# Seven block products in place of eight in one output stage

## The chip, the core and the metric

The kernel runs on one NeuronCore of a Trainium2 chip. The core has a matrix engine (TensorE, PE in the profile, with PEld for its weight loads), a vector engine (VectorE, DVE), a scalar engine (ScalarE, ACT), a general-purpose engine (GpSimd, POOL) and a queue engine (SyncE, SP). Sixteen DMA engines move data within the on-chip memory SBUF and between it and DRAM (matmul results lie in a separate memory, PSUM); the engine that issues a transfer waits first for what the transfer needs. Each engine works through its own instructions in the order in which the program gives them, and engines wait for each other by semaphores.

The metric is the device time of one execution in microseconds (us), given as the median of several runs.

## The reference

The input x has 2048 rows (time steps) of 512 bf16 numbers. With xn the layer norm of x over each row, the output is

```
out = x + y(xn) + f(xn)
y   = 2 Re( h C^T ) + xn * Dskip     with  h[t] = Lam_bar * h[t-1] + B_bar xn[t]     (512 complex states)
f   = ( silu(xn Wg) * (xn Wu) ) Wd                                                    (512 -> 1376 -> 512)
```

All matrices are bf16. Only one product of these is touched by the change: the product of the states h (real and imaginary part side by side, 1024 numbers for each time step) with the folded output matrix, for one quarter of the time steps.

## The kernel before

The 2048 rows are worked in four chunks of 512 time steps (c = 0 to 3), each chunk in four tiles of 128 rows (n = 0 to 15). For a chunk there are these stages:

- `bproj_chunk(c)`: eight tiles of 128 states by 512 steps (real and imaginary part of 512 states), each four matmuls (L380), copied out of PSUM by ScalarE (L382).
- On VectorE, queued as small steps in a backlog: a rotation (L390, L400, L404), eight scans (L422) and a rotation back, which writes the states of the chunk to the tile `wt` (a tensor of 128 x 2 x 4 x 512: the state's row in its block, real or imaginary part, four blocks of 128 states, 512 steps).
- `gateup_chunk(c)`: eleven column tiles of the gate and up products (L455, and L513 for a last mixed tile); ScalarE applies silu to the one (L474) and copies the other (L475), VectorE multiplies two tiles at a time (L470).
- `out_chunk(c)` and, for chunks 2 and 3 together, `out_pair(2)`: for each of four row tiles ten matmuls with the down matrix into one PSUM bank (`out_ffn`, L592, L566), then the remaining 96 rows of the down product (`out_rows`, L555), then `out_ssm` (L604): eight matmuls of 128 x 512 into the same bank, the states in `wt` against the folded output matrix `CF` (128 x 2 x 4 x 512).

The order on each engine is what the program's order of calls makes of it: the code is recorded in this order and is not reordered. The stages around the change follow each other so: `bproj_chunk(2)`, `out_chunk(0)`, `gateup_chunk(2)`, `bproj_chunk(3)`, `load_rows()`, `out_chunk(1)`, `gateup_chunk(3)`, `out_pair(2)`. VectorE's backlog is worked off between the matmul stages by `pump`, which is given the estimated time of the matmuls just recorded; `need(tag)` empties it up to a tag, and `multiply` records the waiting L470 products.

Three shared resources matter here.

PSUM has eight banks, and every matmul group takes one. `out_chunk(0)` leaves its four banks unfinished: the rest of its down product is added only in `out_chunk(1)`, by `out_rows`. So from `out_chunk(0)` to `out_chunk(1)` four banks are left for all other products. In `out_chunk(1)`, the eight banks hold the eight row tiles of chunks 0 and 1; after `out_rows` ScalarE empties the four of chunk 0 (`out_leave`, L617), and after `out_ssm` those of chunk 1.

POOL's queue issues the transfers that add to what is at the destination, and small moves: 48 moves that lay the last 96 gate-times-up rows into `gu_rows` (L188, twelve for each chunk; those of chunks 0 to 2 are issued one after the other), the four loads of `load_rows` (L182), which bring the last 96 rows of the down matrix into a part of the then unused tile `BT` (called `wd_rows` in the code, and read by `out_rows`), and the output stores that add to DRAM (L618, L542). The transfers of this queue use eight semaphores in turn, and POOL issues one only when the transfer eight places earlier has landed.

SBUF tiles that are free by the second half are `CT` (the raw output matrix), `part_end` and `jidx` (float tables), and three buffers `cm`.

Of the kernel before, what the change touches and what calls it, by code (L numbers as in the profile page):

```python
# [10 lines left out]
F32 = mybir.dt.float32  # L11
BF16 = mybir.dt.bfloat16
ALU = mybir.AluOpType
ACT = mybir.ActivationFunctionType
# [9 lines left out]
def kernel(  # L24
# [17 lines left out]
    nc = tc.nc  # L42
    _, L, D = A_x.shape
# [4 lines left out]
    HW = CW // 2  # L48
    NT = L // 128
    NCH = L // CW  # L50
    TPC = CW // 128
    KD = D // 128
    HK = KD // 2
    NQ = Pst // 128
# [11 lines left out]
    ssm = ctx.enter_context(tc.tile_pool(name="ssm", bufs=1))  # L66
    gut = ctx.enter_context(tc.tile_pool(name="gut", bufs=2))
    up_p = ctx.enter_context(tc.tile_pool(name="up_p", bufs=4))
    opool = ctx.enter_context(tc.tile_pool(name="opool", bufs=6))
# [4 lines left out]
    def bank(shape=(128, CW), dtype=F32):  # L74
        return psum.tile(list(shape), dtype, name="ps")

    def flat(ap3):
        return ap3.rearrange("p q j -> p (q j)")

    x_v = A_x[0].rearrange("(n p) d -> p n d", p=128)  # L80
    out_v = out[0].rearrange("(n p) d -> p n d", p=128)
# [17 lines left out]
    CT = const.tile([128, 2, NQ, D], BF16, name="CT")  # L99
# [3 lines left out]
    CF = const.tile([128, 2, NQ, D], BF16, name="CF")  # L103
# [12 lines left out]
    HD = D // 2  # L116
# [51 lines left out]
    jidx = const.tile([128, CW], F32, name="jidx")  # L168
# [7 lines left out]
    part_end = const.tile([128, D], F32, name="part_end")  # L176
# [95 lines left out]
    V = nc.vector  # L272
# [99 lines left out]
    u_tiles, w_tiles = {}, {}  # L372
    car = {}

    def bproj_tile(c, part, q):
        if c not in u_tiles:
            u_tiles[c] = ssm.tile([128, 2, NQ, CW], BF16, name="u16", bufs=2)
        ps = bank()
        for k in range(KD):
            nc.tensor.matmul(ps[:], lhsT=BT[:, part, k, q * 128:(q + 1) * 128], rhs=xnT[:, k, c * CW:(c + 1) * CW],  # L380
                             start=(k == 0), stop=(k == KD - 1))
        nc.scalar.copy(out=u_tiles[c][:, part, q, :], in_=ps[:])  # L382
# [65 lines left out]
    gu_tiles = {}  # L448
# [9 lines left out]
    def gu_tile(c):  # L458
        if c not in gu_tiles:
            gu_tiles[c] = gut.tile([128, FT - 1, CW], BF16, name="guT")  # L460
        return gu_tiles[c]

    def u_tile(c, fi):
        if (c, fi // 2) not in u_pair:
            u_pair[c, fi // 2] = up_p.tile([128, 2, CW], BF16, name="u2")
        return u_pair[c, fi // 2]

    def product(c, fi):
        g, u = gu_tile(c)[:, fi - 1:fi + 1, :], u_tile(c, fi)[:]
        products.append(lambda: V.tensor_tensor(out=g, in0=g, in1=u, op=ALU.mult))  # L470
# [50 lines left out]
    def gateup_tile(c, fi):  # L521
        if fi == FT - 1:
            return gateup_last(c)
        psg = bank()
        gu_mm(psg, wg_g, c, fi, 0, CW)
        psu = bank()
        gu_mm(psu, wu_g, c, fi, 0, CW)
        gu_out(c, fi, psg, psu)
# [16 lines left out]
    o_tiles = {}  # L545

    def out_blocks(n):

        return ((0, D // 2), (D // 2, D - 128), (D - 128, D)) if n == NT - 1 else ((0, D),)

    def out_rows(c, step):

        for i in range(TPC):
            n, rows = c * TPC + i, slice(i * RT, (i + 1) * RT)
            nc.tensor.matmul(o_tiles[n][0][:], lhsT=gu_rows[c][rows, step, :], rhs=wd_rows[rows, step, :],  # L555
                             start=False, stop=(step == 2 and (c == 0 or n == NT - 1)))

    def out_pair(c):

        multiply(0)  # L560
        for n in range(c * TPC, (c + 2) * TPC):
            o = bank()
            o_tiles[n] = [o]
            k, i = divmod(n, TPC)
            for fi in range(FT - 1):
                nc.tensor.matmul(o[:], lhsT=gu_tiles[k][:, fi, i * 128:(i + 1) * 128], rhs=wd_sb[:, fi, :],  # L566
                                 start=(fi == 0), stop=False)
            pump(FT * 0.2163)
        for step in range(3):
            for k in (c, c + 1):  # L570
                out_rows(k, step)
        need(f"ssm{c}")
        need("skip")
        for n in range(c * TPC, (c + 1) * TPC):
            out_ssm(n)
            pump(2 * NQ * 0.2163)
        need(f"ssm{c + 1}")
        n = NT - 1
        o = o_tiles[n][0]
        V.tensor_tensor(out=part_end[:], in0=o[:], in1=xn_end[:, TPC - 1, :], op=ALU.add)  # L580
        o_tiles[n] = [bank((128, hi - lo)) for lo, hi in out_blocks(n)]
        for n in range((c + 1) * TPC, (c + 2) * TPC):
            out_ssm(n)

    def out_ffn(n):
        c, i = divmod(n, TPC)
        o_tiles[n] = []
        for lo, hi in out_blocks(n):
            o = bank((128, hi - lo))
            o_tiles[n].append(o)  # L590
            for fi in range(FT - 1):
                nc.tensor.matmul(o[:], lhsT=gu_tiles[c][:, fi, i * 128:(i + 1) * 128], rhs=wd_sb[:, fi, lo:hi],  # L592
                                 start=(fi == 0), stop=False)

    def out_ssm(n):
        c, i = divmod(n, TPC)
        if c > 0:
            res = opool.tile([128, D], BF16, name="res")
        for o, (lo, hi) in zip(o_tiles[n], out_blocks(n)):
            fresh = n == NT - 1  # L600
            o = o[:, 0:hi - lo]
            for part in range(2):
                for q in range(NQ):
                    nc.tensor.matmul(o, lhsT=w_tiles[c][:, part, q, i * 128:(i + 1) * 128],  # L604
                                     rhs=CF[:, part, q, lo:hi], start=(fresh and part == 0 and q == 0),
                                     stop=(c > 0 and part == 1 and q == NQ - 1))
            if c == NCH - 1:
                rest = part_end[:, lo:hi] if fresh else xn_end[:, i, lo:hi]
                V.tensor_tensor(out=res[:, lo:hi], in0=o, in1=rest, op=ALU.add)  # L609
                for a, b in ((0, D // 2), (D // 2, D)) if i == 0 else ((lo, hi),):  # L610
                    late = b == D and n in (NT - TPC, NT - 1)
                    (nc.sync if late else nc.scalar).dma_start(out=out_v[:, n, a:b], in_=res[:, a:b])
            elif c > 0:
                out_leave(n, o, res)

    def out_leave(n, o, res):
        nc.scalar.copy(out=res[:], in_=o[:])  # L617
        nc.gpsimd.dma_start(out=out_v[:, n, :], in_=res[:], accum_op=ALU.add)  # L618
# [3 lines left out]
    backlog = []  # L622
    owed = [0.0]
# [9 lines left out]
    def step():  # L633
        for item in backlog[0:AHEAD + 1]:
            if item[2] is not None:
                item[2]()
                item[2] = None
        cost, op, _, _ = backlog.pop(0)
        op()
        owed[0] -= cost  # L640

    def pump(us):

        owed[0] += us
        while backlog and owed[0] >= backlog[0][0] * 0.5:
            step()
        if not backlog:
            owed[0] = 0.0

    def multiply(keep):  # L650

        while len(products) > keep:
            products.pop(0)()
            owed[0] -= 0.65

    def need(tag):

        while any(item[3] == tag for item in backlog):
            step()
# [135 lines left out]
    for fis in (range(4, EARLY - 1), range(EARLY - 1, EARLY)):  # L795
        ps, n = bank(), len(fis)
# [4 lines left out]
        pump(GU * n / 4)  # L801
        multiply(1)

    def bproj_chunk(c):
        need(f"ln{c}")
        for part in range(2):
            for q in range(NQ):
                bproj_tile(c, part, q)
                pump(BP)
                multiply(0 if q else 1)  # L810

    def gateup_chunk(c):
        for fi in [FT - 1, *range(FT - 1)]:
            gateup_tile(c, fi)
            pump(GU)
            multiply(1)

    def out_chunk(c):

        multiply(0)  # L820
        for n in range(c * TPC, (c + 1) * TPC):
            out_ffn(n)
            pump(FT * 0.2163)
        if c == 0:
            need("ln3")
            up_halves()
            multiply(0)
        if c == 1:
            for step in range(3):
                for k in range(2):  # L830
                    out_rows(k, step)
            for n in range(TPC):
                out_leave(n, o_tiles[n][0], opool.tile([128, D], BF16, name="res"))
        need(f"ssm{c}")
        need("cf")
        for n in range(c * TPC, (c + 1) * TPC):
            out_ssm(n)
            pump(2 * NQ * 0.2163)
# [12 lines left out]
    def queue_ssm(c):  # L851
        fwd, back = ssm_ops(c)
        queue(f"ssm{c}", fwd + back)
# [31 lines left out]
    nc.sync.dma_start(out=out[0, 0:(NT - TPC) * 128, :], in_=A_x[0, 0:(NT - TPC) * 128, :])  # L885
    queue_ssm(2)
    out_chunk(0)
    gateup_chunk(2)
    bproj_chunk(3)
    load_rows()  # L890
    for c in range(NCH):
# [36 lines left out]
```

## Time and profile before

| | |
|---|---|
| time, median of 3 runs | 178.35 us (178.13, 178.35, 178.47) |
| span of the profiled execution (first to last instruction) | 176.8 us; the profile gives no other time of that execution |
| time outside the span, by the median | 1.5 us |
| TensorE busy | 172.1 us (97%) |
| VectorE busy | 153.8 us (87%) |
| ScalarE busy | 96.4 us (55%) |
| POOL busy | 51.8 us (29%) |
| `gateup_chunk(2)` | 81.2 to 99.4 us |
| `bproj_chunk(3)` | 99.4 to 106.3 us |
| `out_chunk(1)`: down product, `out_rows`, `out_ssm` | 106.3 to 114.8, to 116.3, 116.5 to 123.3 us |
| granted TensorE clock | full (1.000) |

Times in the profile are microseconds from the start of the span. A line of the timeline gives the start, the duration, the engine, the source line, the operation, output and inputs, how many instructions are merged (x), and in brackets how long the engine had been idle and for what it had waited. For POOL the duration of a transfer's line is the time that POOL needs to issue it, not the time of the transfer; the time from issue to landing stands in the list of transfers.

### The profile page before, as it was taken

How to read it: one execution, taken by the hardware profiler on the slowest of the kernel's cores; microseconds unless marked ns; L12 is line 12 of the kernel's file. 1: busy time of each engine (PE TensorE's matmuls, PEld its weight loads, DVE VectorE, ACT ScalarE, POOL GpSimd, SP SyncE). 2: the span in 40 equal slices, each digit the busy share in tenths (PEclk: the TensorE clock that was granted, in tenths of full speed). 3: DMA queues.
4: the chain of work that ended last, by engine and by line, in shares of the span. 5: the costliest groups of instructions: out<-in, count | busy, mean ns of one | idle time of the engine just before them, and what ended most of it. 6: DMA issues, size and time to landing. Idle time of an engine off the chain costs nothing.

```text
span 176.8 us, 2598 instructions
## 1 busy us (share of the span) xinstructions
PE 172.1 (97%) x939; PEld 83.4 (47%) x954; DVE 153.8 (87%) x235; ACT 96.4 (55%) x178; POOL 51.8 (29%) x86
## 2 busy tenths in 40 slices
PE   8999999999999999999999999999999999999993
PEld 3877544444444444444444444444444444444443
DVE  4779998999999997999999999999999999981033
ACT  5397899867698679714666661053866610001300
POOL 6050120001400220019998040058476510001410
PEclk9999999999999999999999999999999999999999
DMA  5998497995431013900000020029799300000652
GB/s 164 305 186 197 91 247 97 336 272 117 88 73 21 0 30 89 356 4 17 17 19 19 0 85 7 0 23 126 88 126 188 64 6 0 0 4 0 64 99 75
DMA packets 31292, 16.36 MB, mean 92 GB/s; under 512 B 20208, under 2 KB 31088, under 8 KB 31248
## 3 DMA queue, kind: packets, MB, share of 16 engines
q1 hardware_dynamic: 24704, 11.51, 27.5%
q0 software_dynamic: 5184, 4.07, 16.0%
q10 hardware_dynamic: 1392, 0.62, 1.2%
q8 instruction: 7, 0.11, 0.3%
q14 instruction: 5, 0.04, 0.1%
HBM read 8.33 MB, written 5.24 MB: 77 GB/s over the span
## 4 chain that ended last, share of the span: by engine, by line
PE 94%; DMA 2%; issue 1%; SPq 0%; DVE 0%
PE ps L455 35%; PE ps L604 16%; PE ps L380 16%; PE ps L566 10%; PE ps L592 10%; DMA wu<-in_B_w_up_dram 2%; PE ps L693 2%; PE ps L513 2%; PE ps L774 2%; PE ps L555 2%; PE ps L502 1%; PE ps L245 0%; SPq L113 0%; SPq L123 0%; DVE res L609 0%
## 5 line engine op out<-in xcount | busy, mean ns | idle before, releaser
L455 PE MATMUL ps<-xnT,wu 128*128 128x512 bf16 (+1 forms) x144 | 36.3, 373 | 0.2
L455 PE MATMUL ps<-xnT,wg 128*128 128x512 bf16 (+1 forms) x145 | 36.3, 373 | 0.2
L422 DVE TENSOR_TENSOR_SCAN g<-r_t,car,u 128x512 bf16<-128x512 f32 x24 | 28.8, 1263 | 0.0
L380 PE MATMUL ps<-xnT,BT 128*128 128x512 bf16 x126 | 28.2, 379 | 0.1
L604 PE MATMUL ps<-CF,wt 128*128 128x512 bf16 (+2 forms) x140 | 27.6, 355 | 0.4 <-issue 0.3
L474 ACT ACTIVATE guT<-ps 128x512 bf16<-128x512 f32 (+1 forms) x40 | 23.6, 590 | 5.9 <-PE ps L455 5.8
L475 ACT CAST u<-ps 128x512 bf16<-128x512 f32 (+1 forms) x40 | 23.0, 576 | 6.5 <-PE ps L455 6.4
L617 ACT CAST res<-ps 128x512 bf16<-128x512 f32 x12 | 6.7, 590 | 36.1 <-PE ps L604 26.8
L455 PEld LDWEIGHTS <-wu 128*128 128x128 bf16 x148 | 14.5, 98 | 16.6
L188 POOL DMA_DIRECT2D gu_rows<-ul x36 | 17.7, 499 | 15.8 <-DVE ul L490 15.8
L455 PEld LDWEIGHTS <-wg 128*128 128x128 bf16 x148 | 14.4, 98 | 16.5
L382 ACT CAST u<-ps 128x512 bf16<-128x512 f32 x32 | 18.2, 586 | 6.0 <-PE ps L380 5.9
L618 POOL DMA_DIRECT2D out_dram<-res x12 | 10.5, 1221 | 36.2 <-ACT res L617 36.1
L604 PEld LDWEIGHTS <-wt 128*128 128x128 bf16 x144 | 13.3, 98 | 15.0 <-issue 1.3
L380 PEld LDWEIGHTS <-BT 128*128 128x128 bf16 x128 | 12.5, 98 | 14.9 <-issue 0.3
L214 POOL TENSOR_TENSOR rstd<-ve,neg_half 128x2 f32<-128x2 f32 (+1 forms) x4 | 5.7, 1418 | 44.9 <-DVE ve L213 44.9
L592 PE MATMUL ps<-wd_sb,guT 128*128 128x512 bf16 x79 | 17.5, 379 | 0.1
L566 PE MATMUL ps<-wd_sb,guT 128*128 128x512 bf16 x79 | 17.4, 379 | 0.1
L470 DVE TENSOR_TENSOR guT<-guT,u 128x1024 bf16<-128x1024 bf16 x20 | 13.4, 678 | 0.0
L566 PEld LDWEIGHTS <-guT 128*128 128x128 bf16 x80 | 7.8, 98 | 9.5
L592 PEld LDWEIGHTS <-guT 128*128 128x128 bf16 x80 | 7.8, 98 | 9.5
L205 DVE BATCH_NORM_STATS2 stats<-xall 128x6 f32<-128x512 bf16 x14 | 9.5, 678 | 2.7 <-DMA xall<-in_A_x_dram 2.7
(125 smaller groups left out, 201.4 us busy)
## 6 DMA issues: line engine op xcount, KB each, us to landing
out_dram<-in_A_x_dram SPq DMA_DIRECT2D x1, 1536.0 KB, 6.9
out_dram<-res POOLq DMA_DIRECT2D x12, 128.0 KB, 3.5
out_dram<-xall POOLq DMA_DIRECT2D x3, 512.0 KB, 8.4
wd_sb<-in_B_w_down_dram SPq DMA_DIRECT2D x2, 640.0 KB, 8.2
xall<-in_A_x_dram SPq DMA_DIRECT2D x1, 1024.0 KB, 7.1
gu_rows<-ul POOLq DMA_DIRECT2D x36, 8.0 KB, 1.6
wg<-in_B_w_gate_dram SPq DMA_DIRECT2D x1, 512.0 KB, 4.7
wu<-in_B_w_up_dram SPq DMA_DIRECT2D x1, 512.0 KB, 5.5
```

The source lines that it names most:

```text
L188: nc.gpsimd.dma_start(out=gu_rows[c][i * RT:(i + 1) * RT, p, :], in_=product[p * RT:(p + 1) * RT, i * 128:(i + 1) * 128])
L380: nc.tensor.matmul(ps[:], lhsT=BT[:, part, k, q * 128:(q + 1) * 128], rhs=xnT[:, k, c * CW:(c + 1) * CW], start=(k == 0), stop=(k == KD - 1))
L382: nc.scalar.copy(out=u_tiles[c][:, part, q, :], in_=ps[:])
L422: V.tensor_tensor_scan(out=g()[:, part, q, :], data0=r_t[:, q:q + 1].to_broadcast([128, CW]), data1=u_tiles[c][:, part, q, :], initial=ini ...
L455: nc.tensor.matmul(ps[:fs, lo:hi], lhsT=wslice(groups, fi, k), rhs=xnT[:, k, c * CW + lo:c * CW + hi], start=(k == 0), stop=(k == KD - 1))
L470: products.append(lambda: V.tensor_tensor(out=g, in0=g, in1=u, op=ALU.mult))
L474: nc.scalar.activation(out=gu_tile(c)[:, fi, 0:hi], in_=psg[:, 0:hi], func=ACT.Silu)
L475: nc.scalar.copy(out=u_tile(c, fi)[:, fi % 2, 0:hi], in_=psu[:, 0:hi])
L566: nc.tensor.matmul(o[:], lhsT=gu_tiles[k][:, fi, i * 128:(i + 1) * 128], rhs=wd_sb[:, fi, :], start=(fi == 0), stop=False)
L592: nc.tensor.matmul(o[:], lhsT=gu_tiles[c][:, fi, i * 128:(i + 1) * 128], rhs=wd_sb[:, fi, lo:hi], start=(fi == 0), stop=False)
L604: nc.tensor.matmul(o, lhsT=w_tiles[c][:, part, q, i * 128:(i + 1) * 128], rhs=CF[:, part, q, lo:hi], start=(fresh and part == 0 and q == 0 ...
L618: nc.gpsimd.dma_start(out=out_v[:, n, :], in_=res[:], accum_op=ALU.add)
```

## The change

Only the state product of chunk 1 (`out_ssm` for n = 4 to 7) is changed; chunks 0, 2 and 3 keep theirs. The product is one of 512 steps x 1024 states with 1024 states x 512 outputs. It is cut into 2 x 2 blocks: A11, A12, A21, A22 are the halves of the steps (256 each) by real and imaginary part, B11, B12, B21, B22 the parts by halves of the outputs (256 each). Strassen's identity in Winograd's form takes seven block products in place of eight, of sums of blocks:

```
S1 = A21 + A22   S2 = S1 - A11   S3 = A11 - A21   S4 = A12 - S2
T1 = B12 - B11   T2 = B22 - T1   T3 = B22 - B12   T4 = T2 - B21
```

What is added:

- The sums of the weights T1 to T4, written over `CT` (`weight_sums`). Each sum starts with a signed copy by ScalarE, in two halves of 128 x 512 elements, and a transfer on POOL's queue that adds the second block. Ten such copies (eight for T1 to T4, two for -B22 in `part_end`) and five transfers (T4 takes two, the second adds B21; signs are chosen so that only additions are needed), each of 128 x 4 x 256 bf16, 256 KB in pieces of 512 bytes. They are recorded two steps after each tile of `gateup_chunk(2)`.
- The sums of the states S1 to S4 (`state_sums`), in the three `cm` buffers and in `jidx`: eight copies and four transfers, recorded one step after each tile of `bproj_chunk(3)`, four after each row tile of `out_ffn`, and the rest before the products; S2 adds S1, and S4 adds S2, in one contiguous piece of 2 KB for each partition.
- The seven block products (`out_ssm_seven`): each eight matmuls of 128 x 256. Four go to banks of their own, three are added to the row tiles' banks.
- ScalarE copies two of the four to SBUF; VectorE forms the sums of the products in four additions of 128 x 512 in f32 and writes the four results (in place of ScalarE's L617) in four more; the stores are unchanged.

On POOL's queue the built program has this order: 24 `gu_rows` moves; the T3 transfer; 12 `gu_rows` moves; T1, T2, T4 first part, T4 second part, S1, S3; the four `wd_rows` loads; S2, S4; then the stores.

```diff
+    BQ = [[CF[:, j, :, h * HD:(h + 1) * HD] for h in range(2)] for j in range(2)]
+    TQ = [CT[:, i // 2, :, (i % 2) * HD:(i % 2 + 1) * HD] for i in range(4)]
+    neg_b22 = part_end[:].bitcast(BF16).rearrange("p (q j) -> p q j", q=NQ)
+    def signed_copy(out, in_, sign):
+        for lo in range(0, NQ, 2):
+            yield lambda lo=lo: nc.scalar.activation(out=out[:, lo:lo + 2], in_=in_[:, lo:lo + 2], func=ACT.Copy,
+                                                     scale=sign)
+    def added(out, in_):
+        yield lambda: nc.gpsimd.dma_start(out=out, in_=in_, accum_op=ALU.add)
+    def weight_sums():
+        (b11, b12), (b21, b22) = BQ
+        t1, t2, t3, t4 = TQ
+        for out, in_, sign, to, add in ((t3, b12, -1.0, t3, b22), (t1, b11, -1.0, t1, b12), (t2, b11, 1.0, t2, t3),
+                                        (t4, b22, -1.0, t4, t1), (neg_b22, b22, -1.0, t4, b21)):
+            yield from signed_copy(out, in_, sign)
+            yield from added(to, add)
...
+    def state_sums(c):
+        (a11, a12), (a21, a22) = state_quarters(c)
+        s1, s2, s3 = (ssm.tile([128, NQ, HW], BF16, name="cm", bufs=3) for _ in range(3))
+        s4 = jidx[:].bitcast(BF16).rearrange("p (q j) -> p q j", q=NQ)
+        s_tiles[c] = (s1, s2, s3, s4)
+        for out, in_, sign, to, add in ((s1, a21, 1.0, s1, a22), (s3, a21, -1.0, s3, a11), (s2, a11, -1.0, s2, s1),
+                                        (s4, a12, -1.0, s4, s2)):
+            yield from signed_copy(out, in_, sign)
+            yield from added(to, add)
+    def out_ssm_seven(c):
...
+        def product(a, b, place, start, stop):
+            for i in range(2):
+                for q in range(NQ):
+                    nc.tensor.matmul(place(i), lhsT=a[:, q, i * 128:(i + 1) * 128], rhs=b[:, q, :],
+                                     start=(start and q == 0), stop=(stop and q == NQ - 1))
...
+        product(a12, b21, at(0, 0), False, False)
+        one = taken(a11, b11)
+        nc.scalar.copy(out=low[:, :, 0], in_=one[:])
+        x = taken(s1, t1)
+        nc.scalar.copy(out=five, in_=x[:])
+        six = taken(s2, t2)
+        step()
+        step()
+        add(u2, six[:], low[:, :, 0])
+        add(low[:, :, 1], u2, five)
+        seven = taken(s3, t3)
+        product(a22, t4, at(1, 0), False, True)
+        product(s4, neg_b22, at(0, 1), False, True)
+        add(high[:, :, 0], seven[:], u2)
+        add(high[:, :, 1], high[:, :, 0], five)
+        finish(1, high)
+        finish(0, low)
+        pump(4 * 2 * NQ * 0.2163)
...
     def bproj_chunk(c):
...
+                spend(1, c == NCH - 1)
     def gateup_chunk(c):
...
+            spend(2)
     def out_chunk(c):
...
+            if c == 1:
+                spend(4, True)
...
         need(f"ssm{c}")
         need("cf")
+        if c == 1:
+            spend(99, True)
+            return out_ssm_seven(c)
...
     out_chunk(0)
+    sums += [*weight_sums(), None]
     gateup_chunk(2)
```

More of the change, by code (lines that the diff above doesn't have):

```diff
@@ new lines, in state_quarters @@
+    def state_quarters(c):
+        w = w_tiles[c]
+        return [[w[:, j, :, h * HW:(h + 1) * HW] for j in range(2)] for h in range(2)]
+    s_tiles = {}
+    def state_sums(c):
[7 more added lines that the diff above has]
+            yield from added(to, add)
@@ new lines, in out_ssm_seven, with at, taken, add @@
+    def out_ssm_seven(c):
+        (a11, a12), (a21, a22) = state_quarters(c)
+        (b11, b12), (b21, b22) = BQ
+        (s1, s2, s3, s4), (t1, t2, t3, t4) = s_tiles[c], TQ
+        first = c * TPC
+        space = flat(gu_tiles[c][:]).bitcast(F32).rearrange("p (s j) -> p s j", j=HD)
+        high, low = (space[:, a:a + 4].rearrange("p (i h) j -> p i h j", h=2) for a in (2, 6))
+        u2, five = high[:, :, 1], space[:, 0:2]
+        def product(a, b, place, start, stop):
[3 more added lines that the diff above has]
+                                     start=(start and q == 0), stop=(stop and q == NQ - 1))
+        def at(half, h):
+            return lambda i: o_tiles[first + 2 * half + i][0][:, h * HD:(h + 1) * HD]
+        def taken(a, b):
+            x = bank((128, 2, HD))
+            product(a, b, lambda i: x[:, i, :], True, True)
+            return x
+        def add(out, in0, in1):
+            V.tensor_tensor(out=out, in0=in0, in1=in1, op=ALU.add)
+            owed[0] -= 0.69
+        def finish(half, extra):
+            for i in range(2):
+                n = first + 2 * half + i
+                res = opool.tile([128, D], BF16, name="res")
+                add(res[:], o_tiles[n][0][:], extra[:, i].rearrange("p h j -> p (h j)"))
+                nc.gpsimd.dma_start(out=out_v[:, n, :], in_=res[:], accum_op=ALU.add)
+        product(a12, b21, at(0, 0), False, False)
[16 more added lines that the diff above has]
+        pump(4 * 2 * NQ * 0.2163)
@@ L802, with spend @@
         multiply(1)
+    sums = []
+    def spend(n, late=False):
+        while n and sums:
+            if sums[0] is None:
+                if not late or any(item[3] == "ssm1" for item in backlog):
+                    return
+                sums[0:1] = state_sums(1)
+            sums.pop(0)()
+            n -= 1
     def bproj_chunk(c):
```

## The prediction

> **What bounds the kernel now.** I read the page's totals first, then the chain that ended last in order of time.
>
> ```profile
> span 176.8 us, 2598 instructions
> ...
> PE 172.1 (97%) x939; PEld 83.4 (47%) x954; DVE 153.8 (87%) x235; ACT 96.4 (55%) x178; POOL 51.8 (29%) x86
> ...
> PE 94%; DMA 2%; issue 1%; SPq 0%; DVE 0%
> ```
>
> ```profile
> 10.52 5.20 PE ps L455 x32
> 15.72 3.13 PE ps L774 x56
> ...
> 99.36 6.91 PE ps L380 x32
> ...
> 107.83 7.07 PE ps L592 x32
> 114.90 1.41 PE ps L555 x24
> 116.31 0.16 issue
> 116.47 6.86 PE ps L604 x31
> 123.32 0.86 PE ps L513 x4
> ...
> 160.29 10.74 PE ps L604 x49
> ```
>
> The columns of the chain are start, duration, and what with how many instructions. TensorE carries the chain from 6 us to the end without a gap over 0.2 us, so a microsecond of matmul time saved, or of stall added, arrives at the end as one. The stage that is changed runs from 116.47 for 6.86 us. VectorE is 87% busy, but holds 0% of the chain: nothing on it is waited for at the end.
>
> **Removed from the path: matmul time.** The chain gives the spacing of back-to-back matmuls by width: 6.91 / 32 = 0.216 us for 512 columns (at 99.36), 5.20 / 32 = 0.1625 for 384 (at 10.52), 3.13 / 56 = 0.056 for 128 (at 15.72). That is proportional to the columns, so 256 columns take 0.108. The stage had 32 x 0.216 = 6.9 us and gets 7 products x 8 matmuls x 0.108 = 6.05: **0.86 us saved**. Each narrow matmul still needs its weights loaded:
>
> ```profile
> L604 PEld LDWEIGHTS <-wt 128*128 128x128 bf16 x144 | 13.3, 98 | 15.0 <-issue 1.3
> ```
>
> 0.098 us is under 0.108, so the loads stay hidden, though barely; were they not, 56 x 0.01 would be the price of each 10 ns. ScalarE's four result copies go, too (they hid beside the matmuls).
>
> **Added: ScalarE's ten weight copies in the gate-and-up stage of chunk 2.** This stage has only four PSUM banks, since the unfinished tiles of chunk 0 hold the others.
>
> ```profile
> 69.84 0.72 ACT L363 ACTIVATE cm<-CT,c2re 128x512 f32<-128x512 bf16 x1
> 70.45 0.72 ACT L363 ACTIVATE cm<-CT,nc2re 128x512 f32<-128x512 bf16 x1
> ...
> 82.13 0.59 ACT L516 ACTIVATE gu_last<-ps 96x512 bf16<-96x512 f32 x1 [6.35 <-PE ps L513]
> 82.74 0.58 ACT L517 CAST ul<-ps 32x512 bf16<-32x512 f32 x1
> 83.34 0.60 ACT L474 ACTIVATE guT<-ps 128x512 bf16<-128x512 f32 x1
> 83.86 0.58 ACT L475 CAST u<-ps 128x512 bf16<-128x512 f32 x1
> 84.72 0.60 ACT L474 ACTIVATE guT<-ps 128x512 bf16<-128x512 f32 x1 [0.28 <-PE ps L455]
> ```
>
> The nearest row to a copy of 512 elements from SBUF is the scaled copy at 69.84: 0.72 us, one every 0.61. Ends: 0.52 (the spacing of L474 to L475, from PSUM) and 0.72 (nothing overlaps); I take 0.61. Today a gate or up result comes every 0.865 us (84.72 less 83.86 agrees) and ScalarE needs 1.10 us of each 1.73 (0.52, then 0.58). Two copies follow L517, so the first silu starts at 83.34 + 1.22 = 84.56; up to the seventh silu lie 6 tiles x 1.10 and 8 copies x 0.61, so it starts at 96.04 and frees its bank at 96.64. TensorE wants that bank for the 17th group after the one that ended at 82.10, at 82.10 + 16 x 0.865 = 95.94. With 0.04 for the semaphore it **stalls 0.74 us**, and after that ScalarE catches up. At 0.52 the bank is free at 95.74: no stall; at 0.72 it costs 1.84. The eight state copies fall into a stage in which ScalarE does 0.58 of each 0.865 and are spread one for each group; the 2 us of lead that four banks give hides them. VectorE's products of gate and up run late anyway:
>
> ```profile
> 92.51 0.68 DVE L470 TENSOR_TENSOR guT<-guT,u 128x1024 bf16<-128x1024 bf16 x1
> ```
>
> The first of this chunk starts at 92.51 without idle time before it, some 5 us after its last input (the second copy after 84.72). Copies later by 2 us do not hold it up.
>
> **Added: nine accumulating transfers in POOL's queue.** These I cost by what stands behind them: the four `wd_rows` loads, which `out_rows` needs at 114.84, are now queued behind seven of them.
>
> ```profile
> 78.72 17.66 POOL L188 DMA_DIRECT2D gu_rows<-ul  x36 [15.82 <-DVE ul L490]
> 102.90 2.20 POOL L182 DMA_DIRECT2D BT<-in_B_w_down_dram  x4 [6.52 <-PE ps L380]
> ...
> 127.24 3.90 POOL L542 DMA_DIRECT2D out_dram<-xall  x3 [2.12 <-DVE xall L536]
> ```
>
> ```profile
> L542 POOL DMA_DIRECT2D out_dram<-xall x3: 1300/1460/1627, 127.2 to 129.5; - x3
> ```
>
> ```profile
> out_dram<-res POOLq DMA_DIRECT2D x1, 128.0 KB, 3.0
> ```
>
> ```profile
> out_dram<-xall POOLq DMA_DIRECT2D x1, 512.0 KB, 6.3
> ```
>
> ```profile
> DMA to landing us min/median/max: 6.3/8.4/9.9
> ```
>
> ```profile
> gu_rows<-ul POOLq DMA_DIRECT2D x36, 8.0 KB, 1.6
> ...
> BT<-in_B_w_down_dram POOLq DMA_DIRECT2D x4, 96.0 KB, 2.8
> ```
>
> ```profile
> q0 software_dynamic: 192, 0.39, 9.8%
> ```
>
> Landing is counted from the start of the issue (last figure of the list's rows; the line with three figures is for the three 512-row transfers). An accumulating transfer of 128 rows, 128 KB, landed after 3.0 us, one of 512 rows, 512 KB, after 6.3. The new ones have 512 pieces but 256 KB. By bytes, between the two rows, they take 4.1 us; by pieces 6.3. Both rows go to DRAM; within SBUF a small move lands after 1.6, so I lean below the middle: **4.8**. Of this 1.46 is POOL's issue (the 512-row transfer's median; one follows another after (129.5 - 127.2) / 2 = 1.15) and 1.6 - 0.5 = 1.1 is the fixed latency of a small move, which leaves 2.25 in the DMA engines; transfers queued together then land 2.25 apart (the 512-row ones, 1.15 apart at issue, landed 1.15 + 8.4 - 6.3 = 3.2 and 1.15 + 9.9 - 8.4 = 2.6 apart, half of which would be 1.4).
>
> Now the queue, all as estimates. T3 is issued after 24 moves x 0.49, at 90.5, and lands at 95.3; the eighth move after it waits for it (the semaphores go round in eight), 0.2 us late, and the twelfth is out at 97.7. T1: 97.7, lands 102.5. T2: 98.9, lands 104.8. The first part of T4 needs T1: 102.5, lands 107.3. The second part must wait for that: 107.3, lands 112.1. POOL stands still meanwhile, and behind it wait S1 (108.5, lands 114.4), S3 (109.6, lands 116.6) and the four loads of `wd_rows`, issued from 110.8 to 113.0, not at 102.90 as before. A load takes the engines 9.8% x 14 us / 4 = 0.34 us, and all four follow S3 in the queue: the last lands at 116.6 + 4 x 0.34 = 118.0 (unqueued, 2.8 after its issue, it would be 115.2 to 115.8).
>
> `out_rows` starts at 114.84 + 0.74 = 115.6; its fourth matmul needs the fourth load, and 21 matmuls x 0.061 (1.47 / 24) follow: end at 119.3 in place of 115.6 + 1.47 = 117.1. **TensorE stalls 2.2 us.** The cover is gone once a transfer takes over about 4.4 us: at 4.1 the last load lands at 114.5 and costs nothing; at 6.3 it lands at 128.2 and costs 12.4.
>
> What is late next: S2 (issued when S1 lands, behind the loads) lands at about 119.5, is needed at 122.0; S4 lands at about 123.4, is needed at 124.6. T4 landed at 112.1. These I cost at nothing, with 1.2 us as the smallest margin. The chunk-0 stores come later; nothing but VectorE's third result (its buffer is that of the first store) waits for them, and by then it has landed.
>
> **Added: eight VectorE operations.**
>
> ```profile
> 118.47 1.22 DVE L390 TENSOR_TENSOR pm<-g,c 128x2048 bf16<-128x2048 bf16 x1
> 119.61 2.35 DVE L390 TENSOR_TENSOR pm<-g,s 128x2048 bf16<-128x2048 bf16 x2
> ...
> 157.45 1.23 DVE L404 TENSOR_TENSOR wt<-pm 128x2048 bf16<-128x2048 bf16 x1
> 160.18 0.69 DVE L580 TENSOR_TENSOR part_end<-ps,xn_end 128x512 f32<-128x512 f32 x1 [1.50 <-PE ps L555]
> 168.90 0.69 DVE L609 TENSOR_TENSOR res<-ps,xn_end 128x512 bf16<-128x512 f32 x1 [8.03 <-PE ps L604]
> ```
>
> Each is like L609: 0.69 us, together 5.5. Their backlog ends with the states of chunk 3, at 157.45 + 1.23 = 158.7, which TensorE uses after the four tiles of chunk 2, at 160.29 + 6.9 = 167.2. So 8.5 us are free. VectorE also waits for the third product: it is ready for it at 119.61 + 1.2 = 120.8, and the product is done at 119.3 + 0.16 + 4 x 0.86 = 122.9, 2.1 us more. 7.6 of 8.5 and TensorE itself is 2 us later: hidden. The banks that the additions empty are taken up in the order in which they come free; the first two come from ScalarE's copies.
>
> **The sum.** -0.86 + 0.74 + 2.2 = +2.1 us. The span of 176.8 becomes 178.9; the median is 1.55 above the profiled span and I keep that: 178.35 + 2.1 = **180.5 us**.
>
> [...]
>
> [...]
>
> ```profile
> L188 POOL DMA_DIRECT2D gu_rows<-ul x36: 496/498/564, 78.7 to 95.9; - x36
> ```
>
> ```profile
> 86.50:91.00 4.50, 4.50 (x23) 2.02 (x21) 4.50 (x7) 3.14 (x6) 4.50 (x10) 1.00 0.08 17
> 91.00:95.50 4.50, 4.50 (x22) 2.06 (x21) 4.50 (x10) 3.13 (x6) 4.50 (x11) 1.00 0.08 19
> ```
>
> The 36 moves were issued in 0.496 to 0.564 us each, while VectorE was busy all the time (in the stretches of 4.50 us the third busy time, after PE and PEld, is VectorE's 4.50), so I add nothing to POOL's issues. [...]
>
> **Rivals.**
> - *The loads stay covered* (the case that is not slower). The place is the fourth `wd_rows` load, the price the 2.2 us, and the point from which it decides 4.4 us for a transfer. For it: both ends lie in SBUF, and a small move there lands after 1.6. Against it: 3.0 us for half the bytes in a quarter of the pieces. The sum is then -0.86 + 0.74: 178.2, no measurable change.
> - *Faster*: the same with cheaper copies. From 0.57 a copy down the stall is under 0.35; at 0.52 nothing is left of it: 177.5. Against it: both rows of copies from SBUF, 0.61.
> - *Pieces count, not bytes.* 6.3 us a transfer: -0.86 + 0.74 + 12.4, 190.6.
> - *Copies at 0.72, loads covered*: -0.86 + 1.84, 179.3.
> - *VectorE becomes the bound*, once more than 8.5 us come before the states of chunk 3. At 0.69 for each addition it does not; were the two f32 additions within SBUF, which no row shows, twice as long, it would be 9.0, which TensorE's own delay still covers. At 12 us it would cost 12 - 8.5 - 2.1 = 1.4 more: 181.9.
> [...]
>
> **Chances.** Forecast, the loads late by 0.5 to 7 us: 0.50 (its own range 178.8 to 185.5). Covered, within 0.2% (about what a measurement of this kernel can tell from no change, 0.36 us): 0.16. Faster: 0.12. By pieces: 0.10. Copies alone: 0.06. VectorE: 0.03. Blocked issues: 0.03. So faster 0.12, same 0.16, slower 0.72. The range leaves out the edge of the faster case and the upper part of the case by pieces: 177.6 to 187.
>
> **What would show it.** In the chain of waits `out_rows` (line 555) waits for a DMA into `BT`, about 2 us, and the first accumulation is issued near 90.5. TensorE shows 0.5 to 1 us of idle time before line 455 between 90 and 97, released by ScalarE. The 56 matmuls of line 610 take 6.05 us, with 0.108 between them; a spacing above 0.11 would make the saving wrong. The list of transfers shows `CT<-CF` landing after 4 to 6 us; under 4.4, or with the loads of `BT` landing before 115, the main term is wrong. VectorE's last L404 ends before TensorE's chunk 3.

## The result, and the profile after

| kernel | median | range | ratio to the kernel before (95% interval) |
|---|---|---|---|
| before | 178.41 us | 178.03 to 179.19 | |
| changed | 183.77 us | 183.27 to 185.59 | 1.032 (1.0285 to 1.0354) |

The change costs 5.4 us. The forecast was 2.1. The direction was right and the time lies in the range given, but the size is off by more than a factor of two.

The totals of the page after:

```profile
span 182.2 us, 2703 instructions
...
PE 176.0 (97%) x978; PEld 86.8 (48%) x978; DVE 159.0 (87%) x243; ACT 102.4 (56%) x194; POOL 62.7 (34%) x95
...
PEclk9999999999999999999999999859999999999999
```

TensorE got seven products in place of eight and yet is busy for 3.9 us longer (172.1 before). The clock row says why: two slices of 4.55 us, the 26th and above all the 27th, are below full clock. The stage lies there. First TensorE's timeline (start, duration, instructions, in brackets the idle time before and its releaser), then the same stretch cut into windows (busy times of PE, PEld, DVE, ACT, POOL, then granted clock, DMA share, GB/s):

```profile
105.77 8.80 PE L685 MATMUL ps<-wd_sb,guT 128*128 128x512 bf16 x40
117.06 4.18 PE L555 MATMUL ps<-BT,gu_rows 32*128 32x512 bf16 x24 [2.50 <-DMA BT<-in_B_w_down_dram]
121.18 3.17 PE L610 MATMUL ps<-CF,wt 128*128 128x256 bf16 x16
124.19 2.78 PE L610 MATMUL ps<-CT,cm 128*128 128x256 bf16 x24
```

```profile
113.00:117.00 4.00, 1.56 (x8) 0.57 (x6) 4.00 (x4) 0.00 (x0) 1.48 (x3) 0.99 1.17 187
117.00:118.00 1.00, 0.94 (x2) 0.20 (x2) 1.00 (x6) 0.00 (x0) 0.00 (x0) 0.50 1.11 184
118.00:120.00 2.00, 2.00 (x18) 0.77 (x20) 2.00 (x5) 0.00 (x0) 0.40 (x1) 0.50 0.09 15
...
122.00:124.00 2.00, 2.00 (x12) 1.48 (x11) 0.00 (x0) 0.51 (x2) 2.00 (x4) 0.56 0.91 106
124.00:126.00 2.00, 2.00 (x21) 1.79 (x19) 0.00 (x0) 1.17 (x2) 0.78 (x1) 1.00 1.06 131
```

Two things happen one after the other. `out_rows` (L555) finds its `wd_rows` missing and TensorE stands still for 2.50 us; this was forecast. Then the clock falls to half just as the first of the four loads arrives, and stays there for 6.8 us; this was not. The chain of waits shows both:

```profile
111.43 6.62 DMA BT<-in_B_w_down_dram
118.06 3.19 PE ps L555 x21
121.24 7.47 PE ps L610 x56
```

Before, all 24 matmuls took 1.41 us; here the last 21 take 3.19 by the chain. But the chain lets them begin at 118.06, where the third matmul starts and the last load has not landed. The times of the four loads from issue to landing, and the weight loads that follow the fourth matmul (timeline), show it:

```profile
DMA to landing us min/median/max: 7.1/7.1/7.3
```

```profile
118.53 0.13 PEld L555 LDWEIGHTS <-gu_rows 32*128 32x128 bf16 x7 [0.40 <-issue]
```

The last load is issued at 111.43 and lands at 118.5; the working said 118.0. So 0.5 us of the 3.19 is still waiting, and from there to the next line pass 2.7 us. POOL's timeline follows the working almost row for row:

```profile
97.82 1.34 POOL L569 DMA_DIRECT2D CT<-CF  x1 [0.22 <-issue]
98.63 1.83 POOL L569 DMA_DIRECT2D CT<-CT  x1
102.64 1.26 POOL L569 DMA_DIRECT2D CT<-CT  x1 [2.17 <-ACT u L382]
107.48 1.27 POOL L569 DMA_DIRECT2D CT<-CF  x1 [3.58 <-DMA CT<-CT]
108.23 3.11 POOL L569 DMA_DIRECT2D cm<-wt  x2
109.73 3.84 POOL L182 DMA_DIRECT2D BT<-in_B_w_down_dram  x4
```

These are T1, T2, the two parts of T4, S1 with S3, and the four loads; the working had 97.7, 98.9, 102.5, 107.3, 108.5 and 110.8.

### The profile page after: what moved, and what is told of

The parts are those of the page before. It is cut to its first block, busy times and chain, and to the rows that moved or that the text cites. A ratio compares the mean times of both kernels' runs of the same rounds, so it can differ in the third digit from the quotient of the medians.

```text
span 182.2 us, 2703 instructions
## 1 busy us (share of the span) xinstructions
PE 176.0 (97%) x978; PEld 86.8 (48%) x978; DVE 159.0 (87%) x243; ACT 102.4 (56%) x194; POOL 62.7 (34%) x95
## 4 chain that ended last, share of the span: by engine, by line
PE 34%; DVE 33%; POOL 14%; DMA 7%; issue 6%; ACT 3%; SPq 1%; POOLq 0%; DVEq 0%
PE ps L659 9%; PE ps L455 9%; POOL gu_rows L188 9%; PE ps L697 8%; DVE pm L390 6%; DVE g L422 5%; DVE stats L205 4%; PE ps L610 4%; DMA BT<-in_B_w_down_dram 4%; DVE guT L470 3%; DVE pm L315 3%; PE ps L555 3%; DMA xall<-in_A_x_dram 2%; POOL CT L569 2%; DVE CF L366 2%
## 5 line engine op out<-in xcount | busy, mean ns | idle before, releaser
L710 ACT CAST res<-ps 128x512 bf16<-128x512 f32 x8 | 4.4, 593 | 35.5 <-PE ps L697 23.3
L188 POOL DMA_DIRECT2D gu_rows<-ul x36 | 18.3, 634 | 15.9 <-DVE ul L490 15.8
L697 PE MATMUL ps<-CF,wt 128*128 128x512 bf16 (+2 forms) x112 | 21.1, 349 | 0.0
L697 PEld LDWEIGHTS <-wt 128*128 128x128 bf16 x112 | 10.2, 98 | 11.1 <-issue 0.8
L711 POOL DMA_DIRECT2D out_dram<-res x8 | 6.9, 1092 | 24.7 <-issue 22.1
```

Source lines behind the costliest of these rows:

```text
L188: nc.gpsimd.dma_start(out=gu_rows[c][i * RT:(i + 1) * RT, p, :], in_=product[p * RT:(p + 1) * RT, i * 128:(i + 1) * 128])
```

## The experiments

The first theory after the result: 5.4 us = -0.9 (products) + a wait for the row loads + half clock that this wait sets off. The rival was that something in the sums or the products themselves is dear (ScalarE's copies, the narrow matmuls, VectorE's additions). Four kernels split the change.

### The row loads taken off POOL's queue

```diff
-            nc.gpsimd.dma_start(out=wd_rows[i * RT:(i + 1) * RT], ...)
+            nc.sync.dma_start(out=wd_rows[i * RT:(i + 1) * RT], ...)
```

> Only the four wd_rows loads move from POOL's queue to SP's. Theory A (the loads stand behind the accumulating transfers, TensorE idles, and its clock then falls): no idle time before line 555, the clock stays at 1.000, and the time is 178.4 - 0.86 = 177.5, at most 178.4 if S4's transfer is late by up to 0.9 us. Theory B (the stage of seven products is itself slow: narrow matmuls, bank waits, VectorE's additions): the time stays above 181. Theory C (the clock falls for some other reason than idle time): the clock still falls to 0.5 near 117 and the time is about 180.

Measured: 179.57 us (179.34 to 180.97) against 178.29 in the same session, ratio 1.009 (1.0055 to 1.0126). Most of the loss is gone and the profiled clock is full, so the loads carried it. But it is 2.1 us above the 177.4 that the products alone give (below), and 1.2 above the most that was expected. TensorE's timeline:

```profile
114.52 1.48 PE L555 MATMUL ps<-BT,gu_rows 32*128 32x512 bf16 x24
...
120.30 1.04 PE L610 MATMUL ps<-CT,wt 128*128 128x256 bf16 x8
122.41 1.03 PE L610 MATMUL ps<-part_end,jidx 128*128 128x256 bf16 x8 [1.07 <-DMA jidx<-cm]
```

`out_rows` no longer waits, and so the last product comes early enough to wait 1.07 us for S4 (`jidx`): the chain S1, S2, S4 of transfers, each of which needs the one before. The last eight matmuls start 2.11 us after the eight before them, which take 0.88: 1.23 us late. One microsecond of idle time did not lower the clock. The remaining microsecond is explained in the part on the end of the span.

### The wait filled with matmuls that add nothing

```diff
+            for _ in range(16):
+                nc.tensor.matmul(o_tiles[7][0][:], lhsT=prm_rows[:], rhs=wd_sb[:, 0, :], start=False, stop=False)
```

> Sixteen matmuls of 128 x 512 with a zero weight are put ahead of out_rows (they add zero to a bank that is being accumulated), so TensorE is busy while it waits for the loads, which land as late as before. Theory A: the wait of about 3.5 us stays, but the clock stays at 1.000; out_rows takes 1.4 us after the last load in place of 3.2 and the 56 matmuls 6.05 in place of 7.47, so the time is 183.8 - 3.2 = 180.5. Theory C: no change, 183.8. If the loss were the load's lateness alone, also 183.8.

Measured: 181.41 us (181.17 to 181.78), ratio 1.0174 (1.0154 to 1.0195). The wait is still there, but TensorE is busy during it, and the clock stays at full. Of the 3.2 us that were expected back, 2.2 came. Chain of waits of this run:

```profile
111.75 7.03 DMA BT<-in_B_w_down_dram
118.78 0.04 issue
118.83 1.45 PE ps L555 x21
120.28 6.22 PE ps L610 x56
```

Same transfers, same landing within 0.3 us, but from the last load to the next line pass 1.45 us in place of 2.7, and 56 matmuls take 6.22 in place of 7.47. Work was added to TensorE, and the kernel became 2.2 us faster than the changed one (5.36 above its own before against 3.12). That is the price of the half clock in the medians; in the two profiled runs it is 2.5. The expectation had counted the whole 3.19, wait included.

### Products alone, sums alone

```diff
 # products alone: no sums, raw blocks in their place
-        (s1, s2, s3, s4), (t1, t2, t3, t4) = s_tiles[c], TQ
+        (s1, s2, s3, s4), (t1, t2, t3, t4) = (a21, a22, a21, a12), (b11, b12, b12, b22)
 # sums alone: made, not used; the product of eight blocks as before
-            return out_ssm_seven(c)
```

> The sums of weights and states are left out (no copies, no accumulating transfers), and the seven products are made of plain blocks in their place, so the output of chunk 1 is not the reference's. Theory A: the stage takes 6.05 us, VectorE's eight additions are hidden, 177.5. Theory B: above 179.

> The sums are made as in the change, but not used: the state product of chunk 1 is the eight-block one of before, with its copies out by ScalarE. Theory A: the loads are late and the clock falls as in the change; 183.8 + 0.86 = 184.6. Theory B: 178.4, as before.

Products alone: 177.43 us (177.25 to 177.91), ratio 0.9952 (0.9936 to 0.9967), so 0.86 us faster. Sums alone: 184.23 us (183.99 to 186.19), ratio 1.0355 (1.030 to 1.041). The loss is whole without any of the new products or VectorE additions. TensorE's timeline of the sums alone:

```profile
118.50 4.20 PE L555 MATMUL ps<-BT,gu_rows 32*128 32x512 bf16 x24 [3.93 <-DMA BT<-in_B_w_down_dram]
```

The wait is longer by 1.4 us, and the clock falls to half again (0.57 from 118 to 120, 0.50 from 120 to 122). The profiled run is the slowest of its four; the other three have a mean clock of 0.991, so less time at half clock than its 0.981. And of the products alone, the chain:

```profile
115.00 1.41 PE ps L555 x24
116.41 6.22 PE ps L610 x56
122.63 0.86 PE ps L513 x4
```

The 56 narrow matmuls take 6.22 us, 0.111 each. So the rival falls: products and additions cost nothing beyond their matmuls.

### Half the filling

```diff
-            for _ in range(16):
+            for _ in range(8):
```

> As the change, with eight zero matmuls (1.73 us) in place of sixteen ahead of out_rows, so that TensorE idles only the last 1.7 to 2 us of its wait for the loads. If any idle time of this size halves the clock, 183.8 as in the change; if the clock stays through 1.7 to 2 us, 181.4 as with sixteen.

Measured: 182.46 us (181.72 to 183.34; the four runs 181.72, 181.76, 183.15, 183.34), ratio 1.023 (1.0194 to 1.0266). The profiled run is one of the two short ones; its timeline:

```profile
114.50 1.89 PE L939 MATMUL ps<-wd_sb,prm_rows 128*128 128x512 bf16 x8
117.35 0.79 PE L555 MATMUL ps<-BT,gu_rows 32*128 32x512 bf16 x2 [0.96 <-DMA BT<-in_B_w_down_dram]
118.30 0.37 PE L555 MATMUL ps<-BT,gu_rows 32*128 32x512 bf16 x1 [0.16 <-DMA BT<-in_B_w_down_dram]
118.83 1.45 PE L555 MATMUL ps<-BT,gu_rows 32*128 32x512 bf16 x21 [0.15 <-DMA BT<-in_B_w_down_dram]
```

About 1.3 us of idle time is left in three parts (1.7 to 2 were expected), and the clock stayed full. Of the two long runs one shows a mean clock of 0.991, by an estimate some 3.3 us at half clock (0.009 x 181.5 / 0.5); the other shows none, and why it is long isn't known. So an idle time of 1.1 to 1.3 us did not lower the clock in the profiled runs, 2.5 us did; where the edge lies between them isn't known.

### The order of the transfers

S1 and S3 do not need T4, but stood behind its second part, which stands still on POOL for 3.58 us (107.48 above). Two kernels issue them ahead of it: one with the loads still on POOL's queue, one with the loads on SP's.

```diff
-            yield from added(to, add)
+            if out is not neg_b22:
+                yield from added(to, add)
...
+            if out is s2:
+                yield from added(TQ[3], BQ[1][0])
```

> The same new order of the sums, with the wd_rows loads left on POOL's queue behind T4's second part, which is now issued at about the same time as before with two transfers fewer behind it. Theory A: the last load lands at 113.5 to 115, so TensorE waits 0 to 0.5 us, without loss of clock: 177.5 to 178.0. If the place in the queue did not matter, 183.8.

> The wd_rows loads go by SP's queue, and the sums S1 and S3 are issued before T4's second part, while POOL waited for T4's first part. Theory A, now with a second wait behind the first (the chain of sums T1, T4, T4, S1, S2, S4 one after the other in one queue, whose last, S4, was late by 1.3 us in the run with the loads on SP): S4 lands about 4 us earlier, no idle time of TensorE before line 610's last eight matmuls, clock 1.000, time 178.35 - 0.86 = 177.5. If the rest of the loss in that run had another cause (copies, VectorE), the time stays at 179.5.

Measured: with the loads on POOL 178.39 us (178.06 to 179.11), ratio 1.0006 (0.9993 to 1.002); with the loads on SP 178.34 (178.01 to 178.89), ratio 1.0002 (0.999 to 1.0014). Five microseconds of loss are gone, but 177.5 to 178.0 was expected of the one and 177.5 of the other. With the loads on POOL they are nearly in time; timeline:

```profile
114.59 0.58 PE L555 MATMUL ps<-BT,gu_rows 32*128 32x512 bf16 x2
115.55 1.94 PE L555 MATMUL ps<-BT,gu_rows 32*128 32x512 bf16 x22 [0.37 <-DMA BT<-in_B_w_down_dram]
117.42 1.92 PE L613 MATMUL ps<-CF,wt 128*128 128x256 bf16 x16
```

From the first of these matmuls to the next line passed 2.83 us in place of 1.41: the rest of the wait eats the saving (this profiled run is 0.6 us above the median). With the loads on SP nothing waits any more; chain:

```profile
114.37 1.41 PE ps L555 x24
115.78 6.22 PE ps L613 x56
122.00 0.86 PE ps L513 x4
```

That leaves the question why 178.34 and not 177.5, with a TensorE that does exactly what it does in the kernel with the products alone.

### The end of the span

TensorE's last matmul started 1.33 us earlier than before in that run, the span ended only 0.5 us earlier (176.3 against 176.8). The difference lies behind the last output store. The start of that store is the last figure of these rows (stores of `res` on SP's queue; the kernel before, then S1 and S3 ahead with the loads on SP):

```profile
L612 SPq DMA_DIRECT2D out_dram<-res x2: 351/359/367, 169.6 to 174.4; - x2
```

```profile
L708 SPq DMA_DIRECT2D out_dram<-res x2: 368/372/375, 168.3 to 173.1; - x2
```

From there to the end of the span pass 2.4 us before and 3.2 in the experiment. At its end the program lets SP wait, one after another, for the completion counter of every kind of transfer. The transfers of SP's and ScalarE's queues take eight counters in turn, as their semaphores in the trace show (before: 101, 102, 111, 112, 113, 115, 116 and 118, in the order in which SP looks at them). In the kernel before, the last store falls on the counter that SP looks at last of these eight; in the experiment it falls on the fourth, and SP looks at four more behind it. From the last landing to the end of the span pass 0.93 us in the one and 1.66 in the other. Two kernels test whether the turn is what counts: the kernel before with nothing changed but the four loads on SP's queue, and the experiment with each of these loads cut into two halves, so that eight transfers are added to these queues and the turn is as before.

```diff
 # kernel before, loads on SP
-            nc.gpsimd.dma_start(out=wd_rows[i * RT:(i + 1) * RT], ...)
+            nc.sync.dma_start(out=wd_rows[i * RT:(i + 1) * RT], ...)
 # order and loads on SP, in halves
+            for h in range(2):
+                nc.sync.dma_start(out=wd_rows[i * RT:(i + 1) * RT, :, h * HD:(h + 1) * HD],
+                                  in_=B_w_down[FL:F, h * HD:(h + 1) * HD].rearrange("(p f) d -> f p d", f=RT))
```

> The kernel before, with nothing changed but the four row loads issued by SP's queue in place of POOL's. They were covered in the kernel before, so TensorE's chain stays as it is. Theory of the counters: the last outputs fall on counters that SP looks at early, and the end of the span comes 0.7 to 0.8 us later behind the last landing: 178.3 + 0.8 = 179.1 us. Rival (the end of e5 has to do with the sums): 178.3 us, and 0.93 us from the last landing to the end.

> As e5 (row loads on SP's queue, S1 and S3 issued ahead of T4's second part), but each of the four row loads on SP is cut into two halves of 256 columns, so eight transfers in place of four. In e5 TensorE's last matmul started 1.33 us earlier than before (172.54 against 173.87), yet the span ended only 0.5 us earlier: from the last output's landing to the end of the span passed 1.66 us (174.65 to 176.31) in place of 0.93 (175.91 to 176.84). At the end SP waits one after another for the completion counters of all transfers; there are eight for the transfers of SP's and ScalarE's queues, taken in turn, and four transfers more on these queues put the last outputs on counters that SP looks at early, so that waits for other counters follow the last landing. Theory: this order is what cost e5 its gain. With eight transfers more the last outputs are on the same counters as in the kernel before, the span ends 0.93 us after the last landing, and the time is 178.34 - 0.8 = 177.5 us. Rival: the longest of these waits (0.49 us, for a counter that had long been reached) is SP's own instruction supply and comes wherever its instructions lie; then 177.8 to 178.1. Second rival: the eight smaller loads land too late for out_rows; then 178.3 or more, with TensorE idle ahead of line 555.

Measured: the kernel before with the loads on SP 179.18 us (179.07 to 179.39) against 178.57, ratio 1.0042 (1.0028 to 1.0056): slower, although nothing was added and TensorE's last matmul ended 0.35 us earlier in the profiled run. The order with halved loads 177.60 us (177.44 to 177.85), ratio **0.9952 (0.9938 to 0.9965)**: it keeps the 0.86 us of the products and beats both kernels. The same row of the two (before with the loads on SP; halved loads):

```profile
L612 SPq DMA_DIRECT2D out_dram<-res x2: 368/370/372, 169.3 to 174.1; - x2
```

```profile
L710 SPq DMA_DIRECT2D out_dram<-res x2: 372/374/375, 168.6 to 173.5; - x2
```

Their spans end at 177.3 and 175.9: 3.2 and 2.4 us after these stores. In the first the last store falls on the fourth counter again, in the second on the last. Both came out as expected, so the order of the counters is shown to be what costs 0.8 us. One part of it stays open: in this row of waits SP stands still once for about 0.5 us, at a counter that had long been reached. It does so in the halved-loads kernel too (174.01 to 174.51), but there the last store is still under way (it landed at 174.94), and nothing is lost.

With this the loads-on-SP experiment nearly closes as well: -0.86 + 1.23 (S4) + 0.8 (the end) = +1.2, measured +1.3.

## Why the prediction was wrong in size

**The sum, as measured.** -0.86 (products alone) + 0 (ScalarE) + 3.98 (the wait: 181.41 less 177.43, both with full clock and in one session) + 2.24 (half clock: 5.36 less 3.12) = +5.36. The prediction had -0.86 + 0.74 + 2.2 and nothing else.

**The step that failed** is the one that turned the wait into time: "a microsecond of matmul time saved, or of stall added, arrives at the end as one". It does not, once the stall lowers TensorE's clock. The working has no term for the clock; the profile of before, which has no such stall, showed it full. 2.5 us of idle time set off 6.8 us of half clock (0.50 from 117 on, and 0.56 between 122 and 124, so up to 123.8), which cost 2.2 us in the median and 2.5 in the profiled run. By an estimate, half clock takes 3.4 us from 6.8 us of matmuls (6.8 / 2); it did not cost that, because up to 118.5 TensorE was still waiting for the other loads. Three of the six runs show a mean clock of 0.991 over some 181.8 us, by an estimate 3.3 us at half clock (0.009 x 181.8 / 0.5), so the stretch was not equally long in all.

What decides is not the length alone. In the sums-alone run TensorE stood idle for 3.7 us before the clock fell (114.6 to 118.27), in the changed kernel for 2.4 (114.57 to 116.95), and in both traces the clock then stayed at half for 6.8 us. With 1.07 us of idle time (loads on SP) and 1.3 us in three parts (half the filling) it stayed full in the profiled runs (1.000). What else decides is not known from these runs.

**The wait for the loads** was mis-sized. Its mechanism was right in each step (order of the queue, the standstill ahead of T4's second part, loads behind S3, 21 matmuls behind the fourth load). Without ScalarE's 0.74 us, which would have covered part of it, the working gives 2.94; it measured 3.98. In the profiled runs of the changed kernel and of the filled one the last load landed at 118.5 and 118.8 where 118.0 was forecast, and TensorE was ready 0.3 and 0.2 us earlier than in the profile of before (its down product starts at 105.77 and 105.94, not 106.11).

**ScalarE's copies** (+0.74) cost nothing. ScalarE's timeline of the changed kernel, and TensorE's where the stall was expected:

```profile
85.13 0.64 ACT L565 ACTIVATE CT<-CF 128x512 bf16<-128x512 bf16 x1
85.66 0.60 ACT L474 ACTIVATE guT<-ps 128x512 bf16<-128x512 f32 x1
```

```profile
94.54 1.03 PE L455 MATMUL ps<-xnT,wu 128*128 128x512 bf16 x4
95.41 1.03 PE L455 MATMUL ps<-xnT,wg 128*128 128x512 bf16 x4
96.27 1.03 PE L455 MATMUL ps<-xnT,wu 128*128 128x512 bf16 x4
```

A copy lasts 0.64 us, but the next instruction starts 0.53 after the copy does, so the two overlap by 0.11. The row taken (0.61, scaled copies) was the wrong one; the other end, 0.52, was nearly right. A silu and its copy, too, took 0.94 to 0.96 us when they followed at once, not 1.10, so the seventh silu started at 94.07, not 96.04. The groups of matmuls follow each other every 0.865 us without a gap.

**The matmuls**: 0.86 was forecast and 0.86 measured, by two errors that cancel in part. 56 matmuls take 6.22 us in place of 6.05 (0.111 each); but the 0.16 us of issue ahead of the stage is gone too, so the chain gives 7.02 - 6.22 = 0.80. The spacing is just above the 0.11 that the forecast had named as a sign against its saving.

**The transfers**: forecast 4.8 us each alone, and late loads only above some 4.4. List of transfers of the changed kernel (KB each, median us to landing):

```profile
CT<-CF POOLq DMA_DIRECT2D x3, 256.0 KB, 4.4
...
CT<-CT POOLq DMA_DIRECT2D x2, 256.0 KB, 5.0
cm<-wt POOLq DMA_DIRECT2D x2, 256.0 KB, 6.8
...
BT<-in_B_w_down_dram POOLq DMA_DIRECT2D x4, 96.0 KB, 7.1
```

These are medians: 4.4 for three transfers with nothing close ahead, 5.0 for one such and one right behind another, 6.8 for the two queued together, 7.1 for the loads behind them (2.8 before). Alone, then, they lie at the edge of 4.4; the loads were late by far more than nothing because each transfer that stood behind another took longer, as the working had it. That rules out the rival by pieces.

**VectorE** is hidden, as forecast:

```profile
126.20 0.69 DVE L622 TENSOR_TENSOR guT<-ps,guT 128x512 f32<-128x512 f32 x1 [5.71 <-PE ps L610]
...
168.08 1.22 DVE L404 TENSOR_TENSOR wt<-pm 128x2048 bf16<-128x2048 bf16 x1
```

The additions take 0.69 us; chunk 3's states are done at 169.3, over 3 us before TensorE's use of them (about 172.4).

**What was costed at nothing.** S4 was given a margin of 1.2 us. In the changed kernel it holds, but only because the stall ahead of it makes TensorE late; without the stall, with the loads on SP, TensorE stands idle for 1.07 us ahead of it. The rival in which the loads stay covered had no such stall either, so its 178.2 may have been too low; no run has transfers as fast as that rival asks.

## What to carry to other kernels

A stall of TensorE in an otherwise dense kernel is not priced by its length alone: from somewhere between 1.3 and 2.5 us on in these runs, add the half clock that may follow it, here 2.2 us; if the stall can't be removed, matmuls that add nothing may keep the clock (with sixteen of them it was 0.998 to 1.000 here). Before transfers are put on a queue, list what stands behind them there and whether one of them makes the queue stand still for a chain: here an order (independent sums first) and another queue for four small loads, each cut in halves, turned +5.4 us into -0.9. And a change of the number of transfers can move the end of the kernel by 0.8 us although no engine's work moved; look at the time from the last store to the end of the span before an expected gain is declared lost.

## What the runs showed of the hardware that was not expected

- TensorE's clock fell to half 2.4 us into an idle time of 2.5 us, and in another run 3.7 us into one of 3.9, each time for 6.8 us in the profiled run; 1.07 us of idle time left it at full.
- Issuing a load of 96 KB from POOL's queue took POOL 0.56 us in the kernel before, and 2.16 us with two accumulating transfers queued ahead of it (median of four each; the four issues still started 0.53 to 0.59 us apart).
- The time from the last store's issue to the end of the span is 2.4 or 3.2 us, by which completion counters the last stores fall on.
